# Transposing the second quarter's pieces ahead of and within the first four feed-forward blocks, and issuing their transfers over eight blocks

## The chip, the cores and the metric

The kernel runs on one core of one Trainium2 chip. The metric is the device time of one execution in microseconds (us), lower is better. The engines are TensorE (PE in the profile; PEld is its weight load), VectorE (DVE), ScalarE (ACT), GpSimd (POOL) and SyncE (SP), whose queue issues all the DMAs of this kernel. Each engine takes its instructions in the order in which the program gives them.

## What is computed

One transformer layer on 2048 tokens of width 448, in float32: layer norm and attention with 16 heads of width 28 that share one key and one value head, then layer norm and a gated feed-forward of width 1792, each with its residual.

```python
h  = x + A(layernorm(x), wq, wk, wv, wo)      # softmax attention, then @ wo
h2 = h + B(layernorm(h), w1, w3, w2)
def B(x, w1, w3, w2):
    return (silu(x @ w1) * (x @ w3)) @ w2
```

## The kernel before

**Split numbers.** Every float32 operand of a matmul is split in a high part (a rounding copy) and a low part (the difference), and each product is three matmuls. `split_w` (L480) does this for the two 448x128 slices of w3 and w1 of one block, with a copy on DVE (L483) and a subtraction on POOL (L484); `split_w2` (L489) does it for the slice of w2 (L496 on DVE, L497 on POOL).

**Feed-forward.** The tokens are four quarters of 512 (`t`), the width 1792 is 14 blocks of 128 (`k`). The main loop (from L1137) runs the 56 blocks `(t, k)`. A block splits the weights of block k+2, runs the matmuls with w3 and w1 on the transposed, normed tokens of the quarter (`ffn1`, or `ffn1_half` in two halves), makes the hidden values (`hidden`: SiLU on ACT, L1033; product on DVE, L1035; high part on ACT, L1040; low part on DVE, L1041), and runs the matmuls of the block before with w2 (`ffn2`, L1071, or `ffn2_half`). The first four blocks of quarter 0 use whole rows of TensorE and have the last quarter's output projection (`wo_rows`, matmuls L166, sum L477) among them; the others use two halves of the rows at a time. Between two halves that write the same bank, `settle` (L1029) reads one number on ACT, and the next half waits for that.

**Transposing a quarter.** Ahead of its own blocks, a quarter's tokens are normed and transposed during the blocks of the quarter before. For each of four pieces `n` of 128 tokens, `ln_norm` (L213, on DVE) writes a tile `xn`, `blocks` (L225, DVE) transposes it in squares of 32x32 into another tile `xn` and puts 16 small copies on a list, and `move(m)` (L238) issues the next m copies of that list as DMAs on SP's queue, each of 16 or 12 KB. They put the squares where they belong in the tile `xh` (a buffer that attention used until its last matmuls). The pool gives out four tiles `xn` in turn, so piece 2 takes the two tiles that piece 0 had, and piece 3 those of piece 1: a transposition into such a tile comes after the 16 DMAs that read it. When all 64 DMAs have landed, `split_x` (L243 on ACT, L247 or L252 on DVE) splits the quarter's transposed tokens, one strip per block, from `(t-1, 9.5)` on.

**Who is called when.** `on(t, k, fn, ...)` puts a call at a place; `call(t, k)` runs the calls of block k behind its `hidden`, and `call(t, k + 0.5)` runs those behind the block's `split_w2`; within a place the order is that of the `on` lines. Also issued on SP in quarter 0, in this order: four DMAs of `rb` in `o_norm` (L449), eight of the last heads' outputs at 0.5 (`o_mul`, L462, which first need the multiplication on DVE, L455), the weights of blocks 6 and 7 at 2.5, of 8 and 9 at 3.5, of 10 to 13 at 4.5, 5.5, 6.5 and 7.5 (`load_w13`: six DMAs a block, L175 to L177), and the slices of w2 (`load_w2`, one DMA, L184): one each at 4.5, 5.5 and 6.5, and three at 7.5.

Of the kernel before, what the change touches and what calls it, by code (L numbers as in the profile page):

```python
# [35 lines left out]
def block_kernel(  # L36
# [18 lines left out]
    def f(ap):  # L55
        return ap.bitcast(F32)
# [150 lines left out]
    def ln_norm(t, n, act=False):  # L207
        _, mv, rs, xns, nb = LN[t]
        xn = xns[n] = ln_pool.tile([P, 512], F32, name="xn", bufs=4)
        if act:  # L210
            se.activation(xn[:, :D], X[t][:, n], AF.Identity, bias=nb[:, n : n + 1], scale=rs[:, n : n + 1])
        else:
            ve.tensor_scalar(xn[:, :D], X[t][:, n], mv[:, n, 0:1], rs[:, n : n + 1],  # L213
                             op0=ALU.subtract, op1=ALU.mult)
# [3 lines left out]
    def xt_tiles():  # L218
        return [xt_pool.tile([P, m, T], F32R, name=name) for m, name in ((4, "xh"), (3, "xl"))]
# [3 lines left out]
    def blocks(t, n):  # L223
        xt = ln_pool.tile([P, 512], F32, name="xn", bufs=4)
        ve.transpose(xt[:, :D], LN[t][3][n][:, :D])  # L225
        if n == 0:
            XT[t] = xt_tiles()
        to = f(XT[t][0])
        x4 = xt.rearrange("i (c b j) -> i c b j", c=4, b=4)
        for a in range(4):  # L230
            for b in range(4):
                m = 4 if b < 2 else 3
                moves.append((to[32 * b : 32 * b + 32, :m, n * P + 32 * a : n * P + 32 * a + 32],
                              x4[32 * a : 32 * a + 32, :m, b]))
# [644 lines left out]
    for s in range(AHEAD, LAST):  # L879
        i, c = divmod(s, NC)  # L880
        n, kt = divmod(c, NQ)
# [221 lines left out]
    def on(t, k, fn, *args):  # L1103
        after.setdefault((t, k), []).append((fn, args))
# [20 lines left out]
    on(0, 12, ln_rstd, tl)  # L1125
    for t in range(1, NT):
        for n in range(NQ):
            k = (1, 3, 4, 6)[n] if t == 1 else 1 + 2 * n
            on(t - 1, k, ln_norm, t, n)
            on(t - 1, k, blocks, t, n)  # L1130
            if t > 1 or n < 2:
                on(t - 1, k, move, 16)
            on(t - 1, 9.5 + n, split_x, t, n)
    for k in range(4, 9):
        on(0, k, move, 7)

    prev = None  # L1137
    for t in range(NT):
# [68 lines left out]
```

## Time and profile before

| | |
|---|---|
| median of 3 runs | 1178.18 us (1177.28 to 1179.29) |
| profiled execution | 1178.61 us, of which the span from first to last instruction is 1176.8 us |
| PE busy | 1150.6 us (98%) |
| DVE, ACT, POOL busy | 806.6, 764.3, 328.9 us |
| mean granted TensorE clock | 0.993 |
| DMA | 34.51 MB, mean 29 GB/s |

The profile is of one execution, and times in it count from the first instruction. A timeline row gives start, duration, engine (SPq is SP's queue), line, operation, output<-input and count; in brackets stands the idle time of the engine before it and what ended that. Attention ends at about 739 us, and the four quarters of the feed-forward follow.

### The profile page before, as it was taken

What the parts mean: (1) busy time and instruction counts of PE and PEld (TensorE: products, weight loads), DVE (VectorE), ACT (ScalarE), POOL (GpSimd) and SP (SyncE); (2) the same over time, 40 slices, a digit from 0 to 9 for tenths busy, and PEclk for the clock granted to TensorE, in tenths of its full rate; (3) what the DMA queues carried; (4) which work ended last, traced back from release to release, by engine and by line L of the source; (5) the groups of instructions that cost most, each with busy time, mean ns of one, the idle gap of its engine ahead of it and who ended that gap; (6) DMA issues with size and microseconds to landing.
All of it is one profiled execution on the core that took longest, in us unless ns stands there. A gap on an engine that the chain in (4) does not pass through costs nothing.

```text
span 1176.8 us, 25851 instructions
## 1 busy us (share of the span) xinstructions
PE 1150.6 (98%) x10154; PEld 772.5 (66%) x10154; DVE 806.6 (69%) x1498; ACT 764.3 (65%) x1587; POOL 328.9 (28%) x242
## 2 busy tenths in 40 slices
PE   8999999999999999999999999999499999999998
PEld 6664444446444445444455443799499999999997
DVE  8878999997999988989988962544253454344333
ACT  5649999996999997999997999312122222222221
POOL 5312001111110111110111013334265555556552
PEclk9999999999999999999999999999799999999999
DMA  4010100001000001100011100223201101100000
GB/s 165 10 37 1 43 12 9 19 22 39 19 19 7 14 24 40 32 20 15 7 40 36 20 18 19 64 68 95 58 33 17 18 1 40 17 9 32 1 2 32
DMA packets 67834, 34.51 MB, mean 29 GB/s; under 512 B 44672, under 2 KB 62336, under 8 KB 67712
## 3 DMA queue, kind: packets, MB, share of 16 engines
q1 hardware_dynamic: 67712, 32.86, 10.6%
q8 instruction: 80, 1.31, 0.5%
q14 instruction: 42, 0.34, 0.1%
HBM read 20.37 MB, written 3.80 MB: 21 GB/s over the span
## 4 chain that ended last, share of the span: by engine, by line
PE 85%; SPq 7%; DVE 2%; ACT 2%; DMA 1%; issue 1%; POOL 0%; ACTq 0%; DVEq 0%; POOLq 0%
PE po L424 20%; PE pb L408 19%; PE pa L1025 16%; PE pa L324 10%; PE pb L1025 8%; PE pb L166 4%; SPq L238 4%; PE po L1025 4%; PE pa L166 3%; SPq L177 1%; SPq L175 1%; ACT OT L431 1%; SPq L176 1%; ACT ab L345 1%; DVE mx L334 1%
## 5 line engine op out<-in xcount | busy, mean ns | idle before, releaser
L334 DVE TENSOR_REDUCE mx<-pa 128x1 f32<-128x512 f32 x689 | 440.2, 685 | 22.2 <-PE pb L408 13.1
L408 PE MATMUL pb<-qs,KS 32*128 32x512 f32 x3072 | 384.8, 425 | 0.0
L415 ACT ACTIVATE pt<-pb 128x512 f32<-128x512 f32 x684 | 366.1, 621 | 20.0 <-PE pb L408 17.3
L408 PEld LDWEIGHTS pb<-qs,KS 32*128 32x128 f32 x3072 | 233.9, 182 | 132.8 <-ACT pt L415 66.9
L324 PE MATMUL pa<-KS,qs 32*128 32x512 f32 x886 | 311.6, 459 | 1.5 <-ACT ab L345 0.2
L1025 PE MATMUL pa<-xl,qs 64*128 64x512 f32 x1044 | 193.6, 389 | 0.0
L324 PEld LDWEIGHTS pa<-KS,qs 32*128 32x128 f32 x886 | 138.6, 182 | 83.2 <-DVE mx L334 46.4
L424 PE MATMUL po<-pt,VA 128*32 128x512 f32 x1368 | 182.2, 604 | 0.4 <-ACT pt L415 0.4
L1025 PE MATMUL pa<-xh,qs 64*128 64x512 f32 x739 | 157.6, 389 | 0.0
L455 POOL TENSOR_TENSOR OT<-OT,rb 128x512 f32<-128x512 f32 x15 | 19.5, 1300 | 458.2 <-DMA rb<-sd 206.9
L1025 PE MATMUL pb<-w2s,pt 64*128 64x448 f32 x1050 | 143.2, 360 | 0.0
L1025 PEld LDWEIGHTS pa<-xl,qs 64*128 64x128 f32 x1044 | 140.2, 185 | 3.2
L1035 DVE TENSOR_TENSOR pt<-pa,pt 128x512 f32<-128x512 f32 x49 | 33.9, 691 | 152.7 <-ACT pt L1033 146.6
L1025 PEld LDWEIGHTS pb<-w2s,pt 64*128 64x128 f32 x1050 | 123.1, 184 | 2.4 <-DVE pt L1041 0.4
L352 DVE CUSTOM_DVE_ANT_0 ab<-pa,ab 128x512 f32<-128x512 f32 x138 | 93.6, 686 | 39.0 <-PE pa L324 27.1
L1025 PEld LDWEIGHTS pa<-xh,qs 64*128 64x128 f32 x739 | 106.7, 185 | 3.1
L415 ACT ACTIVATE xl<-pb 128x512 f32<-128x512 f32 x170 | 99.7, 611 | 9.0 <-PE pb L408 6.8
L415 ACT ACTIVATE xh<-pb 128x512 f32<-128x512 f32 x170 | 104.5, 633 | 0.0
L1033 ACT ACTIVATE pt<-pa 128x512 f32<-128x512 f32 x49 | 29.3, 597 | 96.9 <-PE pa L1025 92.8
L424 PE MATMUL po<-xl,VA 128*32 128x512 f32 x340 | 89.4, 605 | 0.0
L424 PE MATMUL po<-xh,VA 128*32 128x512 f32 x340 | 89.4, 605 | 0.0
L345 ACT ACTIVATE ab<-pa 128x512 f32<-128x512 f32 x138 | 82.2, 608 | 6.5 <-PE pa L324 4.9
(156 smaller groups left out, 1412.9 us busy)
## 6 DMA issues: line engine op xcount, KB each, us to landing
rb<-sd SPq DMA_DIRECT2D x64, 64.0 KB
QR<-OT SPq DMA_DIRECT2D x60, 56.0 KB
QR<-in_B_w_dram SPq DMA_DIRECT2D x16, 192.0 KB
X<-in_A_x_dram SPq DMA_DIRECT2D x3, 896.0 KB
out_dram<-X SPq DMA_DIRECT2D x3, 896.0 KB
xh<-xn SPq DMA_DIRECT2D x128, 16.0 KB
xh<-xn SPq DMA_DIRECT2D x128, 12.0 KB
w<-in_B_w_dram SPq DMA_DIRECT2D x8, 192.0 KB
```

The lines of the kernel that those rows point to most:

```text
L166: pe.matmul(ps, lhs[b][:, cb, lsl], (rhs[2] if ca == 3 and len(rhs) == 3 else rhs[a])[:, ca, rsl], start=(k == 0), stop=(k == len(terms) - 1),
L238: sy.dma_start(*moves.pop(0))
L324: pe.matmul(ps, QS[i][r, 0, n * P : (n + 1) * P], KS[0][r, kt * T : (kt + 1) * T] if keys is None else keys[r], start=True, stop=True)
L334: ve.tensor_reduce(self.to(), ps, axis=AX.X, op=ALU.max)
L345: se.activation(self.ab, ps, AF.Relu)
L352: ve.tensor_tensor_reduce(self.ab, ps, self.ab, 1.0, -3.0e38, ALU.add, ALU.max, self.to())
L408: pe.matmul(self.ps, KS[k % 2][r, c * P : (c + 1) * P], QS[i][r, k // 2], start=(k == 0), stop=(k == 2))
L415: se.activation(f(PT[i, c, p][:, jj]), self.ps, AF.Exp, bias=0.0, scale=SCALE)
L424: pe.matmul(PO[i][32 * j : 32 * j + 32], VA[:, c], f(PT[i, c, j // 2][:, j % 2]), start=(c == 0), stop=(c == NC - 1))
L1025: pe.matmul(ps[:, : rhs.shape[-1]], lhs, rhs, start=bool(first), stop=bool(last), skip_group_check=True)
L1033: se.activation(sg, ps[0], AF.Silu)
L1035: ve.tensor_tensor(sg, ps[1], sg, op=ALU.mult)
```

## The change

Pieces 0 and 1 of quarter 1 are normed and transposed ahead of block 0 (after `o_norm` in the program) where they were at blocks 1 and 3; pieces 2 and 3 go from blocks 4 and 6 to blocks 3 and 3.5. The 64 DMAs, which were 16 at block 1, 16 at block 3, 7 at each of blocks 4 to 7 and the last 4 at block 8, are now 4 at block 0, 12 at 1, 6 at 2, 10 at 3, 12 at 3.5 and 5 at each of blocks 4 to 7. Nothing is added and nothing left out; quarters 2 and 3 keep their places.

```diff
     for t in range(1, NT):
         for n in range(NQ):
-            k = (1, 3, 4, 6)[n] if t == 1 else 1 + 2 * n
-            on(t - 1, k, ln_norm, t, n)
-            on(t - 1, k, blocks, t, n)
-            if t > 1 or n < 2:
+            k = (0, 0, 3, 3.5)[n] if t == 1 else 1 + 2 * n
+            if k:
+                on(t - 1, k, ln_norm, t, n)
+                on(t - 1, k, blocks, t, n)
+            if t > 1:
                 on(t - 1, k, move, 16)
             on(t - 1, 9.5 + n, split_x, t, n)
-    for k in range(4, 9):
-        on(0, k, move, 7)
+    for k, m in ((0, 4), (1, 12), (2, 6), (3, 10), (3.5, 12), (4, 5), (5, 5), (6, 5), (7, 5)):
+        on(0, k, move, m)
+    for n in range(2):
+        ln_norm(1, n)
+        blocks(1, n)
```

## The prediction

> **What bounds the kernel now.** I read the page first (the busy tenths of TensorE and its clock in 40 slices), then the list of waits of PE, then the timeline around the one long wait, then the queue of SP.
>
> ```profile
> PE   8999999999999999999999999999499999999998
> PEclk9999999999999999999999999999799999999999
> ```
>
> ```profile
> PE po L1025 <- ACT pexp L1029: 16.5, 1, 16.5
> PE po L635 <- POOL ident masks.py:199: 1.4, 1, 1.4
> ```
>
> PE is full but for one slice of 29.4 us, the 29th, where its clock is down too. The waits say the same: one wait of 16.5 us, and none over 1.4 beside it. So time is won only by shortening this wait, and lost by any new gap on PE. The timeline shows what the wait is for:
>
> ```profile
> 821.36 1.55 PE L1025 MATMUL pb<-w2s,pt 64*128 64x448 f32 x12
> ...
> 838.68 0.63 ACT L243 ACTIVATE xl<-xh 128x512 fp32r<-128x512 f32 x1 [18.68 <-DMA xh<-xn]
> 839.22 0.14 ACT L1029 ACTIVATE pexp<-po 1x1 f32<-1x1 f32 x1
> ...
> 839.42 0.79 PE L1025 MATMUL po<-xl,qs 64*128 64x512 f32 x1 [16.51 <-ACT pexp L1029]
> ```
>
> PE ends the first half of block 10 at 822.9 (821.36 + 1.55). Its second half waits for `settle` (L1029), which stands on ACT behind the first strip of `split_x` (L243), and that waits for the last of the 64 DMAs xh<-xn. From ACT's start to PE's is 0.74 us. Now the queue that issues them:
>
> ```profile
> 748.72 1.72 SPq L449 DMA_DIRECT2D rb<-sd  x4
> 753.05 6.22 SPq L462 DMA_DIRECT2D QR<-OT  x8
> 759.38 11.31 SPq L238 DMA_DIRECT2D xh<-xn  x16
> ...
> 788.93 0.59 SPq L175 DMA_DIRECT2D OT<-in_B_w_dram  x1
> ...
> 806.44 5.64 SPq L238 DMA_DIRECT2D xh<-xn  x7
> ...
> 834.75 2.59 SPq L238 DMA_DIRECT2D xh<-xn  x4
> ```
>
> ```profile
> 836.74 1.79 DMA xh<-xn
> ```
>
> From 759.38 to 837.34 (834.75 + 2.59) SP issues without a pause: 64 pieces and, by the order of the calls, 54 weight transfers (12 at 2.5, 12 at 3.5, seven at each of 4.5, 5.5 and 6.5, nine at 7.5), 118 in 77.96 us or **0.661 us each**. The chain's row gives 1.79 us from the start of the last issue to its landing, so 1.19 from its end. What bounds this stage is the count of issues ahead of the last piece, not the moment at which a piece is transposed.
>
> **The change, part by part.**
>
> *The queue.* Ahead of QR<-OT the queue is idle from 750.44 (748.72 + 1.72) to 753.05, that is 2.61 us, since QR<-OT needs the multiplication on DVE. The four DMAs now at block 0 go there; four took 2.59 us (row at 834.75). So QR<-OT starts where it did, within 0.1 us, and four issues leave the busy stretch. Were the gap not free, they would cost 2.6 us: I take nothing, the cover being the same gap, and keep 2.6 for the range. The nine weight transfers at 7.5 stood ahead of the last four pieces; now the last piece is issued at block 7, ahead of them. No other issue changes sides: 60 pieces and 45 weight transfers remain, 105 x 0.661 = 69.4 us. The last piece is out 13 x 0.661 = **8.6 us earlier**, at 828.7, the split starts at 830.1 and PE could go on at 839.42 - 8.6 = **830.8**. The nine weight transfers that are now behind it end 9 x 0.661 = 6 us later, at 834.7; the first use of block 13's is at the start of block 11, after block 10's second half, which has yet to run from 830.8. Of the other weight transfers those of block 10 are latest, with 45 pieces ahead of them on the busy stretch where there were 39: 6 x 0.661 = 4.0 us; PE is 7.9 us later by then (below), which covers it. Those of blocks 8 and 9 come four issues earlier, those of 6 and 7 two issues later, against two blocks of lead.
>
> *The transpositions ahead of block 0.* They stand on DVE behind the reciprocal of `o_norm` and ahead of block 0's `split_w`:
>
> ```profile
> 743.70 0.25 DVE L445 RECIPROCAL sm<-sm 128x16 f32<-128x16 f32 x1 [3.79 <-DMA sm<-OT]
> 743.87 0.63 DVE L483 CAST qs<-QR 128x1024 fp32r<-128x1024 f32 x1
> 744.44 0.69 DVE L1035 TENSOR_TENSOR pt<-pa,pt 128x512 f32<-128x512 f32 x1
> 744.58 2.40 POOL L484 TENSOR_TENSOR qs<-QR,qs 128x1024 fp32r<-128x1024 f32 x1 [5.66 <-DVE qs L483]
> ...
> 745.17 0.63 ACT L1040 ACTIVATE pt<-pt 128x512 fp32r<-128x512 f32 x1 [1.35 <-DVE pt L1035]
> ...
> 745.84 1.69 DVE L1041 TENSOR_TENSOR pt<-pt 128x512 fp32r<-128x512 f32 x1 [0.70 <-ACT pt L1040]
> ...
> 749.16 2.57 PE L1071 MATMUL pb<-qs,pt 128*128 128x448 f32 x12
> ...
> 756.66 0.50 DVE L213 TENSOR_SCALAR xn<-X,mv,rs 128x448 f32<-128x448 f32 x1
> 757.19 0.65 DVE L225 STREAM_TRANSPOSE xn<-xn 128x448 f32<-128x448 f32 x1
> 757.76 0.35 DVE L496 CAST w2s<-w2r 128x448 fp32r<-128x448 f32 x1
> ```
>
> A norm and a transposition hold DVE for 1.10 us (756.66 to 757.76), two pairs 2.2 us. All that follows on DVE moves by that: the copy L483 to 746.1, POOL's L484 to 746.8 - 749.2. The low part L1041 ran 1.69 us beside this POOL instruction and ended 0.55 us behind it (747.53 against 746.98); it ended so in the next blocks as well, so it now ends at 749.75. `ffn2` of block 0 starts on PE at 749.16 and takes the low part with its second matmul, about 0.2 us on: PE waits some **0.65 us** (bounds: nothing, if the low part is not held by POOL, and 2.2, the whole shift). Block 2's weights, done at 749.2, are needed behind `ffn2`, at 751.7 (749.16 + 2.57), and stay covered. In blocks 1, 4 and 6 DVE loses work, which gains nothing: it is idle there.
>
> *The transposition of piece 3 at 3.5.* This is the new wait. It writes the tile that piece 1's 16 DMAs read, and the last ten of these are issued at block 3. Ahead of them, from 759.38: 12 + 6 pieces, 12 weight transfers, then the 10, so 40 x 0.661 = 26.4 us; issued by 785.8, or 786.3 at the 0.672 of this very stretch (the 44 issues from 759.38 to 788.93). Landed 1.19 us on, seen by DVE at about **787.5**. Before, DVE was at its next work by 776.2:
>
> ```profile
> 770.23 0.65 DVE L225 STREAM_TRANSPOSE xn<-xn 128x448 f32<-128x448 f32 x1
> ...
> 776.16 0.68 DVE L483 CAST qs<-QR 128x1024 fp32r<-128x1024 f32 x1
> 782.46 0.69 DVE L1035 TENSOR_TENSOR pt<-pa,pt 128x512 f32<-128x512 f32 x1 [5.62 <-ACT pt L1033]
> 783.85 0.69 DVE L1041 TENSOR_TENSOR pt<-pt 128x512 fp32r<-128x512 f32 x1 [0.70 <-ACT pexp L1029]
> ...
> 799.46 0.65 DVE L225 STREAM_TRANSPOSE xn<-xn 128x448 f32<-128x448 f32 x1
> ```
>
> ```profile
> 785.36 1.37 PE L1025 MATMUL pb<-w2s,pt 64*128 64x448 f32 x12
> 786.56 0.86 PE L1025 MATMUL pa<-xl,qs 64*128 64x512 f32 x6
> ...
> 788.83 1.40 PE L1025 MATMUL pb<-w2s,pt 64*128 64x448 f32 x12
> ```
>
> Behind the waiting transposition on DVE stand block 4's copy L483 (776.16 before), the product L1035 (782.46) and the low part L1041 (783.85). From 787.5: 0.6 to the copy (788.1), 0.6 to L1035 (788.7), 1.4 to L1041 (790.1); but POOL's L484 runs from 0.7 behind the copy for 2.4 us, 788.8 to 791.2, and L1041 ends 0.55 behind it, at 791.75. PE wants that low part with the second pair of the matmuls that began at 785.36, so at 785.6, with the shift of block 1 at 786.2: **PE waits 5.6 us** in block 5. Of the wait from 776.7 to 787.5 on DVE, the rest is covered by DVE's own idle time (5.62 ahead of L1035). The transposition of piece 2 at block 3 needs piece 0's 16 DMAs, issued by 759.38 + 12 x 0.661 = 767.3 and landed by 768.5; DVE got to a transposition there at 770.2 and will be no earlier, so no wait.
>
> *The clock.*
>
> ```profile
> 825.00:827.00 2.00, 0.00 (x0) 0.00 (x0) 0.00 (x0) 0.00 (x0) 0.37 (x1) 0.68 0.37 97
> 842.00:843.00 1.00, 1.00 (x8) 0.76 (x8) 0.00 (x0) 0.00 (x0) 1.00 (x1) 0.61 0.00 0
> ```
>
> ```profile
> 843.36 1.37 PE L1025 MATMUL pb<-w2s,pt 64*128 64x448 f32 x12
> ```
>
> In the old gap the granted clock (seventh figure, 0.68 over 825 to 827) fell to half at about 825.7, 2.8 us after PE stopped, and came back at about 842.8. The half block from 839.42 to 843.36 took 3.94 us where the same half took 2.27 (786.56 to 788.83): 1.67 us lost. This goes at block 10 if no long gap is left there. The new wait in block 5, 3.9 us up to the one pair that needs only the high part (L1040, which ended 1.36 us behind the start of L1035, so at 790.1), then 1.7 more, is longer than 2.8 us, so I charge 1.67 there. [...] The measured 2.8 us decides for me; no run here shows a broken gap.
>
> *The sum.* PE comes to block 10's second half at 822.9 + 0.65 + 5.6 + 1.67 = 830.8, and the transfers allow it at 830.8: the two ends meet. Gain 839.42 - 830.8 = 8.6, and 1.67 of slow clock gone there: **10.3 us**. The profiled execution's 1178.61 becomes **1168.3**; that execution is 0.43 above the median of the runs, 1178.18, which gives 1167.9, within the noise. 0.2% (2.4 us) is about what a measurement can tell from no change.
>
> **Rivals.**
>
> 1. *No wait at piece 3* (its tile is free sooner), so no gap in block 5. Then the queue alone decides, PE idles 7 us ahead of block 10 and restarts slow: 8.6 gained, 1178.6 - 8.6 = 1170.0. For it: the row at 799.46 shows no idle time. Against: that piece came 24 issues after the DMAs it needed.
>
> 2. *The four early issues are not free* (they hold QR<-OT back): all of SP is 2.6 later, 1170.9. Against: the gap of 2.61 us.
>
> 3. *Slower: the wait at piece 3 takes in more than its own 16 DMAs.* If what DVE waits for counts the transfers queued behind too, the 12 weight transfers and 12 pieces of 3.5, it ends 24 x 0.661 = 15.9 us later, and PE reaches block 10 at 846.7, where before it was worth 839.42 + 1.67 = 841.1: 5.6 us slower, 1184.2. It decides from a release of DVE later than 797.8. Against: at 799.46 piece 3 was transposed although seven pieces that stand ahead of it in the program were issued only from 806.44. By the 12 weights alone it would be 1176.2, no change to be told.
>
> 4. *The change does nothing:* the last piece still goes out at 837 since the issues, not their places, take the time; 1178.6. Against: nine weights change sides, by the order of the calls.
>
> **How the numbers follow.** Forecast 0.67; rival 1 0.10; rival 2 0.08; rival 3 0.06; rival 4, or rival 3 by the weights alone, 0.05; better than 1166.5, 0.04. Within the forecast: an issue takes 0.648 (2.59 / 4) to 0.707 us (11.31 / 16). The fast pace brings both ends forward by at most 1.4, and without the clock's loss PE follows: 1166.9. The slow one brings the split later by up to 4.8 if it held throughout, which the mean over 118 speaks against; 4 of it, as with the 2.2 of the first blocks and a longer slow clock, gives 1172.3. Range **1166.5 to 1172.5**, which takes in rivals 1 and 2. Faster by over 0.2%: 0.67 + 0.10 + 0.08 + 0.04 = 0.89; within 0.2%: 0.05; slower: 0.06.
>
> **What would show it.** Four rows xh<-xn between rb<-sd and QR<-OT; the last xh<-xn at 827 to 831, ahead of the nine weight transfers; PE waiting 0.3 to 1 us for L1041 at 749 to 750; DVE idle from about 777 to 787 ahead of L225, and PE waiting 4 to 7 us for L1041 in block 5; at block 10 a wait under 2 us. It is wrong if QR<-OT starts later than 754, if L225 starts later than 790, or if another wait over 2 us appears behind block 10.

## The result, and the profile after

The changed kernel takes 1171.36 us (median of 4 runs, 1170.48 to 1172.03), the kernel before 1178.4 beside it: ratio 0.994, 95% interval 0.9923 to 0.9958, so 7.0 us or 0.6% faster. The profiled execution took 1172.03 us with a span of 1170.3. Forecast were 1168.3 and a range of 1166.5 to 1172.5: the way was right, the range held, and the gain of 10.3 us was too large by about 3.

The page after, PE's busy tenths and its clock in 40 slices, then the list of PE's waits:

```profile
PE   8999999999999999999999999999899999999998
PEclk9999999999999999999999999999899999999999
```

```profile
PE po L1025 <- ACT pexp L1029: 5.4, 1, 5.4
PE po L635 <- POOL ident masks.py:199: 1.4, 1, 1.4
PE pb L1025 <- DVE pt L1041: 1.2, 1, 1.2
...
PE pb L1025 <- ACT pexp L1029: 0.6, 1, 0.6
```

The hole in the 29th slice is nearly shut, and the wait of 16.5 us is 5.4. It is the same wait (second half of block 10, behind `settle`, behind the first strip of `split_x`), so the last piece still ends last. SP's queue after, start and duration:

```profile
750.40 1.72 SPq L449 DMA_DIRECT2D rb<-sd  x4
752.23 2.61 SPq L238 DMA_DIRECT2D xh<-xn  x4
754.94 6.25 SPq L462 DMA_DIRECT2D QR<-OT  x8
761.23 12.46 SPq L238 DMA_DIRECT2D xh<-xn  x18
...
781.01 7.46 SPq L238 DMA_DIRECT2D xh<-xn  x10
...
796.11 11.49 SPq L238 DMA_DIRECT2D xh<-xn  x17
...
826.94 3.24 SPq L238 DMA_DIRECT2D xh<-xn  x5
830.23 1.06 SPq L184 DMA_DIRECT2D w_wo<-in_B_w_dram  x2
```

Four pieces stand in the gap behind rb<-sd, and QR<-OT follows them at once. From 761.23 to 830.18 go the 105 issues that the prediction counted, 0.657 us each. The late weights are behind the last piece. Block 10 on ACT and PE:

```profile
831.46 0.63 ACT L243 ACTIVATE xl<-xh 128x512 fp32r<-128x512 f32 x1 [7.50 <-DMA xh<-xn]
```

```profile
825.45 1.37 PE L1025 MATMUL pb<-w2s,pt 64*128 64x448 f32 x12
832.19 0.79 PE L1025 MATMUL po<-xl,qs 64*128 64x512 f32 x1 [5.37 <-ACT pexp L1029]
...
836.62 1.56 PE L1025 MATMUL pb<-w2s,pt 64*128 64x448 f32 x12
```

This execution's attention ended 1.20 us later than the other's, so I count from the copy of the last heads on DVE (L433). Before, and then after:

```profile
739.22 0.69 DVE L433 COPY OT<-po 128x512 f32<-128x512 f32 x1 [1.52 <-PE po L424]
```

```profile
740.42 0.69 DVE L433 COPY OT<-po 128x512 f32<-128x512 f32 x1 [1.52 <-PE po L424]
```

From it to PE's restart in block 10 it was 839.42 - 739.22 = 100.20 us and is 832.19 - 740.42 = 91.77: **8.43 us less**, where 8.6 were forecast from the queue. (The busy stretch of the queue is 9.01 us shorter, but began 0.65 later by this count.) Behind the restart the half block at slow clock took 4.43 us (832.19 to 836.62) where it took 3.94: 0.49 lost, where 1.67 were to be won. That leaves 7.94, and the spans differ by 7.70 from that copy on (437.58 and 429.88). Most of the rest is that the low clock lasted until 837.0 (last section), so that the next matmuls, from 836.62, were slow too: the first group took 1.56 us where it took 1.37.

The other difference to the forecast is on DVE, in block 3:

```profile
777.72 0.50 DVE L213 TENSOR_SCALAR xn<-X,mv,rs 128x448 f32<-128x448 f32 x1
778.26 0.65 DVE L225 STREAM_TRANSPOSE xn<-xn 128x448 f32<-128x448 f32 x1
778.85 0.69 DVE L483 CAST qs<-QR 128x1024 fp32r<-128x1024 f32 x1
```

Piece 3 is transposed at 778.26, with no wait, before the last ten DMAs of piece 1 are even issued (781.01). The wait to 787.5 that the prediction put here does not exist, and so no gap in block 5. This is rival 1, at 1170.0.

### The profile page after: what moved, and what is told of

The parts are those of the page before. It is cut to its first block, busy times and chain, and to the rows that moved or that the text cites. A ratio compares the mean times of both kernels' runs of the same rounds, so it can differ in the third digit from the quotient of the medians.

```text
span 1170.3 us, 25857 instructions
## 1 busy us (share of the span) xinstructions
PE 1153.5 (99%) x10154; PEld 775.4 (66%) x10154; DVE 807.4 (69%) x1498; ACT 764.4 (65%) x1587; POOL 328.7 (28%) x242
## 4 chain that ended last, share of the span: by engine, by line
PE 88%; SPq 5%; DVE 2%; ACT 2%; issue 1%; DMA 1%; POOL 0%; ACTq 0%; DVEq 0%; POOLq 0%
PE po L424 20%; PE pb L408 19%; PE pa L1025 16%; PE pa L324 10%; PE pb L1025 8%; PE pa L166 4%; PE pb L166 4%; PE po L1025 3%; SPq L238 3%; PE pb L1071 1%; DVE mx L334 1%; ACT OT L431 1%; ACT ab L345 1%; SPq L177 1%; SPq L175 1%
## 5 line engine op out<-in xcount | busy, mean ns | idle before, releaser
L1025 PE MATMUL pa<-xl,qs 64*128 64x512 f32 x1044 | 196.9, 389 | 0.0
L1025 PE MATMUL pa<-xh,qs 64*128 64x512 f32 x739 | 160.8, 389 | 0.0
L1025 PEld LDWEIGHTS pa<-xl,qs 64*128 64x128 f32 x1044 | 142.6, 185 | 3.3
```

Of the source, the lines that this page charges most:

```text
L1025: pe.matmul(ps[:, : rhs.shape[-1]], lhs, rhs, start=bool(first), stop=bool(last), skip_group_check=True)
```

## The experiments

**The theories.** *Q*: the stage lasts as long as SP needs for the issues ahead of the last piece, plus landing, up to where `split_x` reads; a transposition's place only decides which issues can go early. *P*: the places of the transpositions on DVE made the gain. *S against A*: whether a new gap ahead of block 10 costs nothing (slack) or its length. *T*: the transfers, not their issues, fill the time. The first four kernels ran on one chip (before: 1179.05), the second four on another (before: 1179.39).

### The last four pieces ahead of the nine weights, nothing else

```diff
-    for k in range(4, 9):
-        on(0, k, move, 7)
+    for k, m in ((4, 7), (5, 7), (6, 7), (7, 11)):
+        on(0, k, move, m)
```

> The kernel before with one edit: the last four pieces are issued at block 7, ahead of the nine weight transfers, and none at block 8; all transpositions stay where they were. If the queue's count decides (theory Q), nine issues leave the front of the last piece: 9 x 0.661 = 5.9 us, so 1172.5 us, with the split on ACT starting about 5.9 us earlier than 838.7. If the places of the transpositions decide (rival P), no change: 1178.4.

Measured 1173.17 us (1171.34 to 1174.02; ratio 0.9953, 0.9939 to 0.9967): 5.9 less, as Q had it. SP's queue and ACT in this kernel:

```profile
822.75 7.09 SPq L238 DMA_DIRECT2D xh<-xn  x11
829.88 1.06 SPq L184 DMA_DIRECT2D w_wo<-in_B_w_dram  x2
```

```profile
831.12 0.63 ACT L243 ACTIVATE xl<-xh 128x512 fp32r<-128x512 f32 x1 [11.13 <-DMA xh<-xn]
```

The split starts 7.6 us earlier than 838.68. The nine issues account for 5.9 of that, and a quicker pace in this execution for the rest (109 issues from 759.30 to 829.84, 0.647 each where it was 0.661). All transpositions stood where they were, so P falls for this part: two thirds or more of the gain need none of them moved.

### One piece transposed early, four DMAs in the gap, nothing else

```diff
-            k = (1, 3, 4, 6)[n] if t == 1 else 1 + 2 * n
+            k = (0, 3, 4, 6)[n] if t == 1 else 1 + 2 * n
...
+    on(0, 0, move, 4)
+    on(0, 1, move, 12)
...
+    ln_norm(1, 0)
+    blocks(1, 0)
```

> The kernel before with one edit: piece 0 is transposed ahead of block 0 and its first four DMAs stand at block 0, in the gap of SP's queue; the other 60 stand where they were. Theory Q: four issues leave the busy stretch, 2.6 us less, 1175.8. With the first experiment the two parts then sum to the whole (5.9 + 2.6 = 8.5). If the gap was not free, 1178.4; if the 1.1 us on DVE ahead of block 0 reached the end, 1179.

Measured 1175.71 us (ratio 0.9976, 0.9966 to 0.9986): 3.3 less, with 2.6 inside the interval (1.7 to 4.0). The gap was free: in this kernel's trace QR<-OT starts 13.92 us behind the copy of the last heads (752.94 - 739.02), where it was 13.83.

### The wait of the prediction, made real

```diff
+    XQ = {}
...
     def blocks(t, n):
-        xt = ln_pool.tile([P, 512], F32, name="xn", bufs=4)
+        if (t, n) == (1, 3):
+            xt = XQ[1, 1]
+        else:
+            xt = XQ[t, n] = ln_pool.tile([P, 512], F32, name="xn", bufs=4)
```

> The changed kernel with one edit: the transposition of piece 3 writes the tile that piece 1's DMAs read, so that the wait exists which the prediction took for granted. In the changed kernel's trace the last of these DMAs lands at about 789.7, so L225 would start there and not at 778.3, and PE would wait about 7 us in block 5. If the 5.4 us ahead of block 10 are slack (theory S), this wait eats them and leaves 1.5 us plus a slow clock in block 5, while the slow restart at block 10 goes: 1170.5 to 1173. If every new gap on PE adds to the end (rival A), 1171.4 + 7 = 1178.

Measured 1170.97 us (1168.83 to 1172.17; ratio 0.9931, 0.9919 to 0.9944), the changed kernel's time within the runs' spread. DVE and PE in this kernel (five lines were added, so L230 is the transposition, L1030 the matmuls, L1034 `settle`, L1046 the low part):

```profile
787.55 0.65 DVE L230 STREAM_TRANSPOSE xn<-xn 128x448 f32<-128x448 f32 x1 [10.69 <-DMA xh<-xn]
788.12 0.65 DVE L488 CAST qs<-QR 128x1024 fp32r<-128x1024 f32 x1
788.69 0.68 DVE L1040 TENSOR_TENSOR pt<-pa,pt 128x512 f32<-128x512 f32 x1
790.07 1.68 DVE L1046 TENSOR_TENSOR pt<-pt 128x512 fp32r<-128x512 f32 x1 [0.70 <-ACT pexp L1034]
```

```profile
790.14 0.74 PE L1030 MATMUL pb<-w2s,pt 64*128 64x448 f32 x2 [4.41 <-ACT pexp L1034]
791.80 2.23 PE L1030 MATMUL pb<-w2s,pt 64*128 64x448 f32 x10 [0.92 <-DVE pt L1046]
```

With the wait in place, the prediction's chain comes true to 0.1 us: transposition at 787.5, copy at 788.1, product at 788.7, low part from 790.1 to 791.75, PE held in block 5 for 4.41 + 0.92 = 5.3 us where 5.6 were worked out. PE comes to the second half of block 10 at 831.15, without a wait, where 830.8 was worked out. The expectation beside the experiment was further off, 789.7 and 7 us: it came from the changed kernel's profiled execution, whose attention ended 1.4 us later than this one's and whose queue was slower up to there. The clock cost more than the 1.67 charged:

```profile
789.00:790.00 1.00, 0.00 (x0) 0.00 (x0) 0.37 (x1) 0.60 (x2) 1.00 (x1) 0.88 0.29 71
796.00:797.00 1.00, 1.00 (x10) 0.81 (x8) 0.00 (x0) 0.00 (x0) 0.00 (x0) 0.70 0.10 15
```

It was at half from 789.76 to 796.60, so PE worked at it for some 5.5 us, where the old gap had 3.4. PE's waits no longer hold the one for the last piece: the gap has only moved from block 10 to block 5, and the time has not. S holds and A falls. So the mechanism was drawn rightly and its condition wrongly: in the changed kernel the tile is another one.

### The split one block later

```diff
-            on(t - 1, 9.5 + n, split_x, t, n)
+            on(t - 1, min(10.5 + n, 12.5) if t == 1 else 9.5 + n, split_x, t, n)
```

> The changed kernel with one edit: the four strips of quarter 1 are split at 10.5, 11.5, 12.5 and 12.5 where they were at 9.5 to 12.5. The last piece then has 7.2 us more, over the 5.4 that PE waits. If the wait for the last piece is all that is left (theory Q), the 5.4 us and the 2.2 of slow clock behind it go, but for some 0.6 that block 13's weights may hold back: 1164.4. If the late weight transfers stop PE as well (rival W), PE waits several us for block 13's weights and little is won: 1169 to 1171.

Measured 1165.4 us (1162.26 to 1166.92; ratio 0.9881, 0.9866 to 0.9896). This median lies between two pairs of runs: 1162.26 and 1163.97 us at a mean clock of 1.000, 1166.83 and 1166.92 at 0.995 and 0.997. The trace is of the run with 1163.97; what held the other pair is not shown. In the trace the wait for the last piece is gone. What stands in its place on PE, and DVE ahead of it:

```profile
816.81 1.28 PE L1025 MATMUL pb<-w2s,pt 64*128 64x448 f32 x10 [1.22 <-DVE pt L1041]
...
832.30 1.27 PE L1025 MATMUL pb<-w2s,pt 64*128 64x448 f32 x10 [0.74 <-DVE pt L1041]
```

```profile
813.07 0.69 DVE L483 CAST qs<-w 128x1024 fp32r<-128x1024 f32 x1 [3.60 <-DMA w<-in_B_w_dram]
...
828.52 0.70 DVE L483 CAST qs<-w 128x1024 fp32r<-128x1024 f32 x1 [4.00 <-DMA w<-in_B_w_dram]
```

Both are the low part on DVE, late since the block's `split_w` ahead of it waited for late weights, by the order of the queue those of blocks 10 and 12. The first was in the changed kernel already, hidden by the gap at block 10; the second is new, at 0.7 us. Rival W had several us for the weights of block 13: DVE waits 2.02 us for them at 835.94, and PE not at all. So W falls, though a late transfer can cost PE a little.

### Twelve weight transfers on ACT's queue

```diff
-    def load_w13(k):
+    def load_w13(k, q=sy):
...
-        on(0, 2.5, load_w13, 2 * tl + k)
+        on(0, 3, load_w13, 2 * tl + k, se)
```

> The changed kernel with one edit: the 12 weight transfers of blocks 6 and 7 are issued on ACT's queue at block 3, where ACT is idle, and no longer on SP's. Theory Q: 12 issues leave the front of the last piece, 12 x 0.661 = 7.9 us, more than the 5.4 that PE waits; then the wait, the 2.2 us of slow clock behind it and the 1.8 us of small waits for late weights ahead of it all go: 1171.4 - 9.4 = 1162. If the transfers themselves and not their issues take the time (rival T), a second queue wins nothing: 1171.

Measured 1162.22 us (1160.72 to 1165.35; ratio 0.9859, 0.9844 to 0.9874). The same DMAs move the same bytes, only issued elsewhere, and the time falls by 8.3 against the changed kernel run beside it (below): Q, and T falls. On SP the last piece goes 93 issues behind QR<-OT. The traced run was the slowest of the four, at 1165.35, and in it a part of the wait is left. Its 93 issues took 0.679 us each, in all 1.7 us more than at 0.661:

```profile
PE po L1025 <- ACT pexp L1029: 1.8, 1, 1.8
```

### The kernel before, with the split alone moved

```diff
-            on(t - 1, 9.5 + n, split_x, t, n)
+            on(t - 1, (11.5, 11.5, 12.5, 12.5)[n] if t == 1 else 9.5 + n, split_x, t, n)
```

> The kernel before with one edit: quarter 1's strips are split at 11.5, 11.5, 12.5 and 12.5; queue and transpositions as before. The last piece lands at 838.5 there, PE's second half of block 12 would start at 837.3 without a wait. If the wait for the last piece is all that the change worked on (theory Q), moving the reader does more than moving the issues: a wait of about 3 us is left of 16.5, and no slow clock: 1164. If the early transpositions are needed for the gain (rival P), it stays above 1170.

Measured 1165.14 us (1164.07 to 1166.29; ratio 0.9883, 0.9868 to 0.9898). Queue and transpositions are those of the kernel before, and yet it is 5 us faster than the changed kernel: P falls for good. What is left on PE are two waits of 1.2 us for the low part, as above; the wait of 3 us that was expected for the last piece is not there.

### The changed kernel again, and both edits

> The changed kernel once more, beside the others on one chip: 1171 to 1172. If the first two experiments are the whole of the change, its gain is their sum, 5.9 + 3.3 = 9.2, less the longer share of slow clock (0.5), so 1170.4; if they overlap, it is nearer to 1172.

Measured 1170.5 us (1170.13 to 1171.56; ratio 0.9928, 0.9915 to 0.994), 8.9 less than before on this chip. The two parts, 5.9 and 3.3 on the other chip, add up to it within the intervals; the first comparison gave 7.0 for the whole.

> The changed kernel with both edits: the 12 weight transfers on ACT's queue and the later split. If the one alone already frees PE from the last piece, the other adds nothing: the same as with ACT's queue alone, 1162 within 1 us. If single late weights still hold PE back, up to 1 us less.

Measured 1160.7 us (1160.51 to 1163.71; ratio 0.9849, 0.9835 to 0.9862), the fastest of all, 1.5 under ACT's queue alone, with overlapping ranges. The longest of PE's waits lie ahead of the feed-forward, which is left with one of 0.2 us, for the low part of block 0:

```profile
PE po L635 <- POOL ident masks.py:199: 1.4, 1, 1.4
PE pb L262 <- ACT xn L211: 1.1, 1, 1.1
...
PE pb L1071 <- DVE pt L1041: 0.2, 1, 0.2
```

It is 18.7 us faster than before; the old gap and the slow clock behind it were 16.5 + 1.67 = 18.2.

## Why the prediction was right, and where it was not

- **What bounds the stage: right.** The count of issues ahead of the last piece, times the pace. 118 issues took 77.96 us before, 105 took 68.95 after; the restart came 8.43 us earlier for 8.6 worked out. The two halves of this (nine weights, four in the gap) were shown apart.
- **The four early DMAs: right, but for some tenths.** The gap took them, in 2.61 us for 2.59. "Within 0.1 us" was too close: QR<-OT starts at 754.94, which is 14.52 us behind the copy of the last heads and was 13.83, so 0.69 later. Of this, 0.36 is a later multiplication (its end, 754.58, is later by that much), and the rest is the queue, busy until 754.84. In the next two kernels with the early four and all else of the change it was 0.2 later. The limit of 754 that the prediction set for being wrong is kept by this count (753.74), though not by the trace's own clock.
- **The transpositions ahead of block 0: right in kind, too large.** PE lost 0.34 us and not 0.65, as its second matmul came 0.54 behind the first where the step is 0.2:

```profile
750.36 0.37 PE L1071 MATMUL pb<-qs,pt 128*128 128x448 f32 x1
750.90 2.48 PE L1071 MATMUL pb<-qs,pt 128*128 128x448 f32 x11 [0.18 <-DVE pt L1041]
```

  The 0.65 does not follow from its own figures: the low part at 749.75 and the second matmul at 749.36 (749.16 + 0.2) are 0.4 apart. All of it was given back at block 10.
- **"It writes the tile that piece 1's 16 DMAs read": wrong, and the step that failed.** I took the four tiles as given out in turn in the changed kernel too. Its trace shows a transposition ahead of the DMAs it should have waited for, so it wrote another tile. In the program's list of instructions, piece 3's transposition writes the tile of piece 2's normed tokens, which is free as soon as piece 2 is transposed. In the list of the kernel before it does write piece 1's tile, as the text on that kernel says; the row at 799.46 has no idle time because those DMAs, issued by 788.93, had long landed. (Some 15 issues had gone out since by the rows of the queue, not 24.) Both lists fit a pool that gives out the tile whose last use comes first in the program: transposing pieces 0 and 1 together changed that order. No run tests this rule by itself. So the row could not tell the two apart, and I gave rival 1, which is what happened, only 0.10.
- **The slow clock: the term that was lost with it.** With a gap left at block 10 of 5.4 us (7 in rival 1), the restart was slow: instead of 1.67 won, 0.49 lost on that half block, 2.16 in all. This is most of the 10.3 - 7.7 between forecast and trace. The sum with the wait (1168.3) and the sum without it (1170.0) happen to differ by under 2 us; that is why the range held, and it is luck, since the path through the blocks was another one than forecast.
- **Late weights: the size right, the cover wrong.** Those of block 10 were issued 4.1 us later for 4.0, but PE was not 7.9 us later, as the wait in block 5 was missing. DVE waits for them, and PE behind it for 0.64 us (at 816.63) and 1.21 us (at 818.31); both went into the slack ahead of block 10:

```profile
814.57 0.69 DVE L483 CAST qs<-w 128x1024 fp32r<-128x1024 f32 x1 [3.64 <-DMA w<-in_B_w_dram]
...
816.56 1.70 DVE L1041 TENSOR_TENSOR pt<-pt 128x512 fp32r<-128x512 f32 x1 [0.70 <-ACT pexp L1029]
```

- **Rivals 2, 3 and 4** did not occur: QR<-OT was held back by tenths and not by 2.6 us, the transposition of piece 3 did not wait at all, and the order of the queue was the gain.

## What to carry to other kernels

When one queue issues without a pause up to a wait, count the issues ahead of what is waited for: here an issue took about 0.66 us, and a piece of 12 or 16 KB no less than a weight transfer of 32 to 224 KB (in the kernel before 0.65 to 0.81 in the groups of pieces, 0.58 to 0.73 in those of weights). Moving issues behind the deadline (5.9 us here), into an idle stretch of the queue (3.3) or to an idle engine's queue (8.3) gave that time back, as long as the wait lasted. Ask also whether the reader can come later: moving one reader by two blocks won 14.3 us where the whole change of the transfers won 8.9 on the same chip. Before a wait is forecast from a buffer's reuse, find out which buffer the pool really gives, since the wait and its cost stand or fall with it.

## What the runs showed of the hardware

The lengths of four stretches of half clock lie close to multiples of one time. Rows of one microsecond each (seventh figure the granted clock) that hold the begin and the end of three of them, in the kernel before, after, and with the last four pieces moved:

```profile
825.00:826.00 1.00, 0.00 (x0) 0.00 (x0) 0.00 (x0) 0.00 (x0) 0.37 (x1) 0.86 0.59 170
842.00:843.00 1.00, 1.00 (x8) 0.76 (x8) 0.00 (x0) 0.00 (x0) 1.00 (x1) 0.61 0.00 0
```

```profile
830.00:831.00 1.00, 0.00 (x0) 0.00 (x0) 0.00 (x0) 0.00 (x0) 0.00 (x0) 0.59 0.15 24
836.00:837.00 1.00, 1.00 (x7) 0.77 (x6) 0.00 (x0) 0.13 (x1) 0.00 (x0) 0.50 0.52 99
837.00:838.00 1.00, 1.00 (x12) 0.94 (x10) 0.50 (x1) 0.47 (x1) 0.00 (x0) 1.00 0.44 165
```

```profile
825.00:826.00 1.00, 0.00 (x0) 0.00 (x0) 0.00 (x0) 0.00 (x0) 0.00 (x0) 0.80 0.08 12
835.00:836.00 1.00, 1.00 (x8) 0.80 (x6) 0.00 (x0) 0.00 (x0) 0.52 (x1) 0.58 0.18 51
```

The rows between these show 0.50, and those outside 1.00. In the kernel before, the steps of 0.1 us show 1.00 up to 825.70, 0.59 in the next and 0.50 behind it; so I take the clock as full or half at every moment, and a mean of 0.86 as full for 0.72 of that microsecond and half for the rest. By this the clock was low from 825.72 to 842.78, 830.18 to 837.0 and 825.60 to 835.84: 17.06, 6.82 and 10.24 us. In block 5 of the kernel with the wait made real it was 6.84 us (789.76 to 796.60). These lengths are within 0.02 us of five, two, three and two times 3.41, a unit that I estimate from them alone (10.24 - 6.82 = 3.42). What sets it, and what decides when the clock falls and comes back, no run shows.

The shorter gap had the dearer restart: PE worked for 3.36 us at the low clock before (842.78 - 839.42) and for 4.8 after (837.0 - 832.19). The half block behind the gap of 16.5 us lost 1.67 us, and the one behind the gap of 5.4 us lost 2.16 (4.43 - 2.27), so here a gap's length alone does not tell the loss. Nor did the fall come at one distance from PE's stop: 2.8 us before (822.9), 3.4 after (826.8) and 4.0 in block 5 of the kernel with the wait made real (785.7).
